# Transposed tokens made by DMA instead of TensorE, and eight score blocks moved ahead

## The chip, the core and the metric

The kernel runs on one core of one Trainium2 chip. The metric is the time of one execution on the device in microseconds (us), lower is better. A core has five engines with a queue of instructions each, which it takes in order: TensorE (PE), VectorE (DVE), ScalarE (ACT), GpSimd (POOL) and SyncE (SP, which here only issues DMAs). An instruction waits for others through semaphores, and everything behind it on its queue waits with it.

## The reference

```python
xn = layernorm(x)                                   # 2048 tokens x 512
a, b = xn @ dft_hid_re.T, xn @ dft_hid_im.T         # spectral part
y = dft_seq_re @ a - dft_seq_im @ b
q = einsum("nd,dhc->nhc", xn, w_q)                  # experts: 32 heads, two halves of 128
s1, s2 = q1 @ k1.T, q2 @ k2.T                       # 64 keys for each half
i1, i2 = the two best keys of s1 and of s2          # for each token and head
top_s, top_e = the two best of the four pairs       # index = 64 * i1 + i2, of 4096 experts
g = softmax(top_s)
act = gelu(xn . u[top_e])
out = x + y + sum over heads and experts of g * act * v[top_e]
```

All inputs and the output are f32.

## The kernel before, in words

The Python builds one straight program. The source says what is done; a scheduler of the framework puts the instructions of each engine in an order, which stays close to the source but moves small work ahead where it can run earlier. Tiles come from pools with a fixed count of buffers, and a new user of a buffer waits until the last one is done. PSUM, where matmuls write, has eight banks: four from `pa`, two from `pb`, two from `pc` (L61 to L68).

**Tokens.** The 2048 tokens lie in eight tiles of 128 partitions by 2 by 512 f32, `xp[0..7]`; `xn(g, q)` (L238) is one block of 128 tokens, and 16 blocks make four groups `g` of four. A group is two tiles, 2g and 2g+1. The same memory seen as f16 is `xt[i]` (L235): per block a high and a low part of 512 columns each, later filled with the transposed tokens. The matmuls of the experts run on two f16 parts: value times 512 (`XS`) as f16, plus what the rounding left.

**Stage 1: normalise.** `ln(g, n)` (L284) takes mean and variance of each token, works out `rstd` and `negm` (L316 to L321), and normalises the block in place on ACT or DVE. One token row of group 0 is kept aside as `x5` and normalised on POOL (L336).

**Stage 2: the spectral part along the sequence.** For each group in the order G = (1, 0, 2, 3), `fold(0, g)` (L360) adds the two tiles (L369) and folds columns (L339 to L358) into Q[0][g] (L372, L373), all on DVE with two small copies on ACT; `main(0, g)` (L394) runs eight f32 matmuls (L403) that add into the four `pa` banks. After the last group `evict(0)` copies the banks out on ACT (L455, L458). The same with differences follows: `fold(1, g)`, `main(1, g)`, `evict(1)`. `fold_row` (L375), `spread` (L385) and the end of `sides` (L438 to L441) treat the single row on POOL, with two small DMAs from POOL's queue (L389, L390); the rest of `sides` (L418) gathers two more columns on DVE.

**Stage 3: key products.** Keys and query weights don't depend on the tokens, so `m_mul` (L136) multiplies them first: for head group j, four heads, the product is `m`, 512 by 512, in four banks. `m_scale(0, ...)` (L187) takes absolute sums of the four banks, of one weight tile and of the keys on ACT (L196 to L201); `pow2` (L115) takes the maximum over all partitions on POOL (`partition_all_reduce`, L118), and DVE makes powers of two out of it (L119 to L124, L206 to L212). `m_parts` (L216) then splits `m` into two f16 parts: the high part on ACT (L219), the low part on DVE (L220), which frees the bank. The argument `at` makes `m_scale` wait for `fold(0, G[-1])`.

**Stage 4: transposes.** `xpose(i, sub)` (L469) transposes one block: four matmuls against the identity into a bank (L475), a scaled copy to f16 on ACT (L478), and the low part either as a further matmul that subtracts the rounded value inside the bank (L480, then L482 on ACT) or as one subtraction on DVE (L484). This happens between `main(1, g)` of the next groups, L549 to L561.

**Stage 5: scores and the best two.** For each of eight head groups j (`NCH`) and each of 16 blocks i, `scores(j, i)` (L773) runs 12 matmuls (L779: four columns of 128 by three products of parts) into a `pa` bank, evicts on ACT (L784), and finds the best eight values of each head with MAX8 and their indices with FIND_INDEX8 on DVE (L787, L791). What else is done between the blocks is a table: `MST0` and `MST` say behind which block each piece of `m_stage(j + 1)` (loads, key products, scale, split) goes, `sums()` (L563) stands behind block 10 of j = 0, `HID` puts the products along the hidden dimension (`y_rows`, `hid` L486) behind blocks 11 to 15 and 27 to 32, and `todo` (L799) the splits of weights (`m_prep`, L151) and the first estimates of u and v (`absmax`, `uv_scale`). During j = 1 each transposed block is also stored to DRAM (`xt_d`, L845). The weights of j are loaded by `m_load` (L131).

**Stage 6: experts.** After the eighth head group the routing is compacted by DMA transposes (L768), all 4096 experts' products with u run densely (L908), then those with v (L991), to the end. The change leaves this stage as it is.

The order of the calls around the change is L502 to L561:

```python
for n, g in enumerate(G):          # L528
    ...
    fold(0, g)
    ...
    main(0, g)
evict(0)                           # L544
m_scale(0, MS[0, "p"], FF[0, G[-1]][:, 0, 0:1])
m_parts(0, MS[0, "p"])
...
for n, g in enumerate(G):          # L549
    fold(1, g)
    ...
    main(1, g)
    if n:
        for q in range(4):
            xpose(4 * G[n - 1] + q, n < 3)
```

## Time and profile before

| what | us |
|---|---|
| median of 3 runs | 1160.65 |
| lowest and highest of them | 1159.43, 1161.57 |
| the profiled execution's own time | 1159.45 |
| span of its trace | 1157.7 |
| TensorE busy in that span | 1136.5 |
| VectorE busy | 934.5 |
| ScalarE busy | 610.6 |
| GpSimd busy | 245.0 |

The span goes from the first to the last instruction of the profiled execution; its own time is that with what lies around it. In the rows of a timeline stand the start in us, the busy time in us, the engine, the line, the operation, the tiles written and read, and how many instructions the row holds; in brackets the idle time before it and what ended that time. In a row of the DMA queues (SPq, POOLq), the three figures are the least, the median and the greatest time of an issue in ns, followed by the stretch in which they stand. In the table of stretches, each pair is the busy time of one engine and its count of instructions, in the order PE, weight loads of PE, DVE, ACT, POOL; then the granted clock of TensorE, the share of the DMA engines and GB/s.

### The profile page before, as it was taken

The page shows a single profiled execution, that of the slowest core. Times are in us where ns is not written, and L with a number is a line of the kernel's source. Part 1 is how long each engine was busy: PE and PEld are TensorE (multiplying, and loading weights), DVE is VectorE, ACT ScalarE, POOL GpSimd, SP SyncE. Part 2 cuts the span into 40 slices and gives each one's busy share as a digit, 9 for nine tenths or more (in the row PEclk, how much of TensorE's full clock was granted, in tenths as well). Part 3 has the DMA queues.
Part 4 walks back from the last instruction along what each step waited for, and adds up shares of the span by engine and source line. Part 5 has one row for each costly group of instructions (what it writes and reads, how often), then busy time and mean ns, then how long its engine had stood idle before and what let it go on. Part 6 is the DMA issues. An engine that isn't in the chain of part 4 may idle for free.

```text
span 1157.7 us, 25371 instructions
## 1 busy us (share of the span) xinstructions
PE 1136.5 (98%) x9930; PEld 724.9 (63%) x9930; DVE 934.5 (81%) x2840; ACT 610.6 (53%) x1056; POOL 245.0 (21%) x232
## 2 busy tenths in 40 slices
PE   6899999999999999999999999999999999999997
PEld 4355555445445459778478479569569559658763
DVE  7987989798898999974994895897886786788670
ACT  5575687687776635354435435535535435433440
POOL 5232464865865410000000000010010000000000
PEclk9999999999999999999999999999999999999999
DMA  9182344243241204261743743644554555451423
GB/s 364 49 294 64 124 139 169 70 164 119 83 159 52 82 11 126 87 213 37 237 157 104 229 166 107 223 159 137 186 163 169 168 174 168 155 174 56 137 75 104
DMA packets 81504, 163.64 MB, mean 141 GB/s; under 512 B 16084, under 2 KB 31323, under 8 KB 81374
## 3 DMA queue, kind: packets, MB, share of 16 engines
q1 hardware_dynamic: 81008, 161.84, 42.2%
q8 instruction: 80, 1.31, 0.5%
q14 instruction: 50, 0.41, 0.1%
q10 hardware_dynamic: 302, 0.08, 0.0%
q0 software_dynamic: 64, 0.00, 0.0%
HBM read 142.69 MB, written 17.63 MB: 138 GB/s over the span
## 4 chain that ended last, share of the span: by engine, by line
PE 93%; DVE 3%; DMA 2%; ACT 1%; issue 0%; POOL 0%; SPq 0%; ACTq 0%; POOLq 0%; DVEq 0%
PE s L779 29%; PE z L908 28%; PE v L991 27%; PE g L946 4%; PE p L403 2%; PE m L144 2%; DVE L L936 1%; PE xp L475 0%; DMA xb<-in_x_dram 0%; DMA x<-in_x_dram 0%; DMA cx<-in_wt_dram 0%; DMA fit<-v_d 0%; DVE act L962 0%; DMA y<-y_d 0%; DVE w L954 0%
## 5 line engine op out<-in xcount | busy, mean ns | idle before, releaser
L908 PE MATMUL z<-xb,u 128*128 128x256 f16 (+1 forms) x3840 | 342.9, 251 | 0.2
L991 PE MATMUL v<-v,act 128*128 128x512 f16 x1536 | 338.6, 379 | 0.0
L908 PEld LDWEIGHTS <-u 128*128 128x128 f16 x3840 | 309.8, 98 | 26.8 <-issue 0.5
L779 PE MATMUL s<-m,xq 128*128 128x512 f16 x1344 | 297.3, 379 | 0.0
L991 PEld LDWEIGHTS <-act 128*128 128x128 f16 x1536 | 147.4, 98 | 171.0
L779 PEld LDWEIGHTS <-xq 128*128 128x128 f16 x1344 | 129.6, 98 | 150.3 <-issue 0.2
L936 DVE TENSOR_TENSOR L<-io_lam,cmp 128x2048 f16<-128x2048 f16 x128 | 155.9, 1218 | 59.1 <-PE g L946 58.9
L915 ACT ACTIVATE act<-z,scl 128x256 f32<-128x256 f32 (+1 forms) x224 | 100.6, 498 | 171.5 <-PE z L908 171.4
L787 DVE MAX8 vals<-ss 128x8 f32<-128x64 f32 x1024 | 152.6, 216 | 12.6 <-ACT ss L784 12.3
L1004 POOL TENSOR_TENSOR y<-y,xr 128x512 f32<-128x512 f32 x15 | 25.2, 1679 | 611.9 <-DMA y<-y_d 455.8
L961 ACT ACTIVATE act<-w 128x1024 f16<-128x1024 f32 x52 | 69.9, 1360 | 92.8 <-DVE w L954 92.1
L791 DVE FIND_INDEX8 idx<-vals,ss 128x8 uint16<-128x256 f32 x256 | 107.2, 419 | 0.0
L954 DVE SCALAR_TENSOR_TENSOR w<-act,scl,g 128x1024 f32<-128x1024 f32 x64 | 80.9, 1274 | 29.7 <-ACT act L915 29.7
L1067 ACT ACTIVATE cx<-cx 128x896 f32<-128x896 f32 x64 | 60.5, 945 | 72.3 <-DVE cx L1047 53.7
L784 ACT ACTIVATE ss<-s,wsc 128x512 f32<-128x512 f32 x112 | 74.7, 680 | 44.3 <-PE s L779 36.6
L962 DVE TENSOR_TENSOR act<-w,act 128x1024 f16<-128x1024 f32 x64 | 84.9, 1328 | 4.2 <-ACT act L961 4.2
L1041 DVE TENSOR_TENSOR cx<-cx 128x512 f32<-128x512 f32 (+2 forms) x84 | 48.4, 610 | 28.0 <-DMA cx<-in_cb_dram 25.0
L946 PEld LDWEIGHTS <-L 128*128 128x128 f16 x2048 | 60.6, 96 | 11.2 <-DVE R L944 1.2
L946 PE MATMUL g<-R,L 128*128 128x32 f16 x2048 | 61.7, 176 | 0.2 <-DVE R L944 0.2
L944 DVE TENSOR_TENSOR R<-R,cmp 128x512 f16<-128x512 f16 x128 | 59.2, 463 | 1.5
L166 POOL TENSOR_TENSOR wq<-wq,wh 128x1024 f16<-128x1024 f32 x26 | 55.4, 2133 | 12.1 <-DVE xq L484 7.9
L941 DVE TENSOR_TENSOR R<-io_c,cmp 128x512 f16<-128x512 f16 x128 | 54.5, 426 | 0.0
(290 smaller groups left out, 1094.3 us busy)
## 6 DMA issues: line engine op xcount, KB each, us to landing
v<-v_d SPq DMA_DIRECT2D x67, 512.0 KB, 4.2
cx<-in_cb_dram SPq DMA_DIRECT2D x64, 448.0 KB, 4.7
wq<-in_wq_dram SPq DMA_DIRECT2D x32, 512.0 KB, 6.0
fit<-in_wq_dram SPq DMA_DIRECT2D x28, 512.0 KB, 5.3
...
```

The costliest lines, as they stand in the source:

```text
L779: nc.tensor.matmul(ps, xt[i][:, l, kd, :], m[:, r, kd, :], start=(n == 0), stop=(n == 3 * KD - 1))
L784: nc.scalar.activation(s.rearrange("p g e -> p (g e)"), ps, AF.Copy, scale=inv)
L787: nc.vector.max(vals[:, i, w, :, h], s[:, g, :])
L791: nc.vector.max_index(idx[:, i, w].rearrange("p k h -> p (k h)"), vals[:, i, w, 0:2].rearrange("p k h -> p (k h)"), s[:, w * HC:g + 1, :]. ...
L908: nc.tensor.matmul(ps if n == 1 else ps.rearrange("p (b n) -> p b n", b=2), ug[:, l, c % 2, kd, :], xb2[:, k0, r, kd, :] if n == 1 else xb ...
L915: nc.scalar.activation(ACT[bb][:, cg * m:cg * m + m, :], pv[:, i], AF.Gelu_apprx_tanh, scale=zsc)
L936: nc.vector.tensor_tensor(L.rearrange("p t (l two) -> p t l two", two=2), io_lam.rearrange("p (l two) -> p l two", two=2).unsqueeze(1).to_ ...
L946: nc.tensor.matmul(p[:, hf, t * NC:(t + 1) * NC], L[:, t, :], R[:, t, :], start=True, stop=True)
L954: nc.vector.scalar_tensor_tensor(w, act[:, :, ts], fw, p.rearrange("p h (n c) -> p c (h n)", c=NC), op0=ALU.mult, op1=ALU.mult)
L961: nc.scalar.activation(w16[..., 0], w, AF.Copy)
L962: nc.vector.tensor_tensor(w16[..., 1], w, w16[..., 0], op=ALU.subtract)
L991: nc.tensor.matmul(pv, w16[:, c, :, l], v_sb[g][:, r, cc, :], start=(n + cc == 0 and k == 0), stop=(n == 15 and cc == 1 and k == 2))
```

## The change

The factor 512 moves into the normalisation: `rstd` is 512 times as large, and where the spectral part leaves the banks (`turn`, `sums`, `spread`), the factor 1/512 is put into the instruction that is there anyway.

The transposes on TensorE go. `stage(i)` takes a block: ACT writes its f16 copy (with a bias of zero from `zs`, which ties it to an earlier step) into one of three staging buffers, DVE writes the difference to it, and one DMA transpose of 128 by 1024 f16, issued by SP, writes both parts to `xt[i]`. The staging buffers are `u_sb[3]` and `u_sb[4]`. The four blocks of group 1 (G[0]) are staged behind `fold(0, 0)`, those of group 0 behind `fold(1, 0)`, those of groups 2 and 3 behind `sides()`, ahead of `evict(1)`. The tokens are overwritten where the transposed tokens land, `xt[i]` in `xp[i // 2]`; for h = 2, 3 (group 1) the tokens now lie in tiles of their own.

The scale and the split of the key products (`m_scale`, `m_parts`) move from behind `evict(0)` to behind `main(0, 0)`, the second of the four sequence products. Behind them stand the first four score blocks, `early(0..3)`, in the banks of `pb` and `pc`, with an eviction on ACT into spare tiles. Four more, `early(4..7)`, stand behind `main(1, 1)`, in the same banks, without an eviction of their own. `scores(0, n)` then takes the blocks in the order TO (group 1, 0, 2, 3), and for n below 8 runs no matmuls: it evicts the bank of blocks 4 to 7 and searches the best values of all. The differences are folded in the order 0, 1, 2, 3 (GK).

Since the matmuls of the first eight blocks are gone from the list of j = 0, the other pieces move back: `MST0` puts the pieces of the key products of j = 1 behind blocks 10 to 15 (4 to 9 before), `absmax` behind 8 and 10, `uv_scale` behind 11, `m_prep` of j = 1 behind 7 to 10. The weights of j = 1 are loaded from POOL's queue, and the last two loads of difference matrices (`load(1, 2)`, `load(1, 3)`) with three small ones stand on SP behind the first four transposes.

```diff
@@ -131,7 +131,7 @@
     def m_load(j, pool, ts):
         for t in ts:
             MS[j, t] = pool(f"wq{j}_{t}")
-            nc.sync.dma_start(MS[j, t], wq[j, t // 2, t % 2])
+            (nc.gpsimd if j == 1 else nc.sync).dma_start(MS[j, t], wq[j, t // 2, t % 2])
...
@@ -238,6 +238,15 @@
     def xn(g, q):
         return xp[2 * g + q // 2][:, q % 2]
+    def s_mm(ps, m, i):
+        n = 0
+        for kd in range(KD):
+            for l, r in ((0, 0), (0, 1), (1, 0)):
+                nc.tensor.matmul(ps, xt[i][:, l, kd, :], m[:, r, kd, :], start=(n == 0),
+                                 stop=(n == 3 * KD - 1))
+                n += 1
+
+
     MP[0] = stS.enter_context(tc.tile_pool(name="mp0", bufs=1, side="left"))
...
     uf = [t.rearrange("p a b k e -> p (a b k e)").bitcast(F32) for t in u_sb]
+    EARLY = {}
+    EV = uf[7].rearrange("p (i w k h) -> p i w k h", i=NT, w=2, k=8)
+    EX = uf[4][:, 512:640].bitcast(U16).rearrange("p (i w k h) -> p i w k h", i=NT, w=2, k=2)
+    ES = uf[4][:, 640:672].rearrange("p (n c) -> p n c", n=4)
+
+    def early(n):
+
+        i = TO[n]
+        m, inv = M[0]
+        ps = (pb if n % 2 else pc)(f"s0_{i}")
+        s_mm(ps, m, i)
+        EARLY[n] = ps, None
+        if n < 4:
+            EARLY[n] = uf[5 + n // 2][:, n % 2 * 512:n % 2 * 512 + 512], ES[:, n]
+            nc.scalar.activation(EARLY[n][0], ps, AF.Copy, scale=inv)
+
     stA = ExitStack()
     da = stA.enter_context(tc.tile_pool(name="da", bufs=1, side="left"))
+    for h in (2, 3):
+        xp[h] = da.tile([P, 2, 512], F32, name=f"x{h}")
+
     def raw_tile(name):
         return da.tile([P, 2, 512], F32, tag="raw", name=name, bufs=10)
     G = (1, 0, 2, 3)
+    GK = G, (0, 1, 2, 3)
...
@@ -316,8 +347,8 @@
         nc.scalar.activation(sm[:, 0], var, AF.Sqrt, bias=eps)
         nc.vector.reciprocal(sm[:, 1], sm[:, 0])
         nc.vector.scalar_tensor_tensor(sm[:, 0], var, 1e-5, sm[:, 1], op0=ALU.add, op1=ALU.mult)
-        nc.vector.scalar_tensor_tensor(sm[:, 2], sm[:, 0], -0.5, sm[:, 1], op0=ALU.mult, op1=ALU.mult)
-        nc.vector.scalar_tensor_tensor(rstd[:, g], sm[:, 2], 1.5, sm[:, 1], op0=ALU.add, op1=ALU.mult)
+        nc.vector.scalar_tensor_tensor(sm[:, 2], sm[:, 0], -0.5 * XS, sm[:, 1], op0=ALU.mult, op1=ALU.mult)
+        nc.vector.scalar_tensor_tensor(rstd[:, g], sm[:, 2], 1.5 * XS, sm[:, 1], op0=ALU.add, op1=ALU.mult)
...
@@ -452,10 +484,10 @@
         d = turned(dst)
         v = halved(src)
         if b is None:
-            nc.scalar.activation(d, v, AF.Copy)
+            nc.scalar.activation(d, v, AF.Copy, scale=1.0 / XS)
             return
         for a in range(2):
-            nc.scalar.activation(d[..., a::2], v[..., a::2], AF.Identity, bias=b[:, a:a + 1])
+            nc.scalar.activation(d[..., a::2], v[..., a::2], AF.Identity, bias=b[:, a:a + 1], scale=1.0 / XS)
     def evict(k):
         PT[k] = [[uf[8 + 2 * k + dt][:, h * 512:(h + 1) * 512] for h in range(2)] for dt in range(2)]
...
@@ -463,25 +495,14 @@
             for h in range(2):
                 turn(PT[k][dt][h], PP[k][dt][h], s5c[:, :, dt] if h + k == 0 else None)
-    idn = cst.tile([P, P], F16, name="idn")
-    nc.gpsimd.tensor_scalar(idn, ident, -1.0 / XS, None, op0=ALU.mult)
-
-    def xpose(i, sub=False):
-
-        p = (pb if sub and i % 2 else pc)(f"xp{i}")
+    def stage(i):
+
         src = xn(i // 4, i % 4)
-        for kd in range(KD):
-            c = slice(kd * P, (kd + 1) * P)
-            nc.tensor.matmul(p[:, c], src[:, c], ident, start=kd == 0, stop=kd == KD - 1 and not sub,
-                             is_transpose=True, skip_group_check=True)
-        pv = p.rearrange("p (k n) -> p k n", k=KD)
-        nc.scalar.activation(xt[i][:, 0], pv, AF.Copy, scale=XS)
-        if sub:
-            nc.tensor.matmul(p, idn, xt[i][:, 0].rearrange("p k n -> p (k n)"), start=False, stop=True,
-                             skip_group_check=True)
-            nc.scalar.activation(xt[i][:, 1], pv, AF.Copy, scale=XS)
-            return
-        nc.vector.scalar_tensor_tensor(xt[i][:, 1], pv, XS, xt[i][:, 0], op0=ALU.mult, op1=ALU.subtract)
+        n = TO.index(i)
+        t = u_sb[3 + n % 3 // 2][:, n % 3 % 2].rearrange("p a k n -> p a (k n)")
+        nc.scalar.activation(t[:, 0], src, AF.Identity, bias=zs[:, int(n > 3):int(n > 3) + 1])
+        nc.vector.tensor_tensor(t[:, 1], src, t[:, 0], op=ALU.subtract)
+        nc.sync.dma_start_transpose(xt[i].rearrange("p a k n -> p (a k) n"), t.rearrange("p a d -> p (a d)"))
     def hid(t, n, pre, pn, pim, bank):
...
@@ -516,13 +537,9 @@
     row512(0, c5r, nc.scalar)
     nc.gpsimd.tensor_copy(c52, c5r[:, 0:2])
     nc.scalar.dma_start(c55, cb[0, 0, 0, 0:1, 8, 0:1])
-    for g in G:
+    for g in GK[1][:2]:
         load(1, g)
     wfs = uf[14][:, 0:512]
-    nc.sync.dma_start(wfs, wf)
-    nc.sync.dma_start(w2, wr[:, 0:2].to_broadcast([P, 2]))
-    row512(1, A[1, 0][0:1, 512:1024])
-
     for t in range(2):
         m_mul(0, t, (0, 1))
     for n, g in enumerate(G):
@@ -531,6 +548,15 @@
         if 0 < n < 3:
             ln(G[n + 1], n + 1)
         fold(0, g)
+        if n == 1:
+            nc.scalar.activation(zs[:, 0:1], rstd[:, g, 0:1], AF.Copy, scale=0.0)
+            for q in range(4):
+                stage(4 * G[0] + q)
+            for h in GK[1][2:]:
+                load(1, h)
+            nc.sync.dma_start(wfs, wf)
+            nc.sync.dma_start(w2, wr[:, 0:2].to_broadcast([P, 2]))
+            row512(1, A[1, 0][0:1, 512:1024])
         if n == 3:
             fold_row(0)
             spread()
@@ -541,24 +567,31 @@
                 m_mul(0, t, (2, 3))
             for t in range(2, 4):
                 m_mul(0, t, range(KD))
+        if n == 1:
+            m_scale(0, MS[0, "p"], FF[0, g][:, 0, 0:1])
+            m_parts(0, MS[0, "p"])
+            nc.scalar.activation(zs[:, 1:2], wsc[:, 0:1], AF.Copy, scale=0.0)
+            nc.scalar.activation(k16[:, 0], k_sb, AF.Copy, scale=sk)
+            nc.vector.scalar_tensor_tensor(k16[:, 1], k_sb, sk, k16[:, 0], op0=ALU.mult, op1=ALU.subtract)
+            for b in range(4):
+                early(b)
     evict(0)
-    m_scale(0, MS[0, "p"], FF[0, G[-1]][:, 0, 0:1])
-    m_parts(0, MS[0, "p"])
-    nc.scalar.activation(k16[:, 0], k_sb, AF.Copy, scale=sk)
-    nc.vector.scalar_tensor_tensor(k16[:, 1], k_sb, sk, k16[:, 0], op0=ALU.mult, op1=ALU.subtract)
-    for n, g in enumerate(G):
+    for g in GK[1]:
         fold(1, g)
         if g == 0:
             nc.vector.tensor_copy(Q[1][0][0:1, 0, 1:256], s5i[:, 1:256])
             nc.scalar.activation(xp[1][0:1], x5, AF.Copy)
+            for q in range(4):
+                stage(q)
         main(1, g)
-        if n:
-            for q in range(4):
-                xpose(4 * G[n - 1] + q, n < 3)
+        if g == 1:
+            for b in range(4, 8):
+                early(b)
     sides()
+    for g in (2, 3):
+        for q in range(4):
+            stage(4 * g + q)
     evict(1)
-    for q in range(4):
-        xpose(4 * G[-1] + q)
     def sums():
         b8 = pc("b8")
...
@@ -770,18 +803,19 @@
             nc.scalar.activation(cmp, zt.unsqueeze(3).to_broadcast([P, 3, P, 2]), AF.Copy)
             CMP[b] = cmp
-        def scores(j, i, vals, idx):
+        def scores(j, n, vals, idx):
             m, inv = M[j]
-            ps = pa(f"s{j}_{i}")
-            n = 0
-            for kd in range(KD):
-                for l, r in ((0, 0), (0, 1), (1, 0)):
-                    nc.tensor.matmul(ps, xt[i][:, l, kd, :], m[:, r, kd, :], start=(n == 0),
-                                     stop=(n == 3 * KD - 1))
-                    n += 1
-            st = sp.tile([P, 520], F32, tag="s", name=f"ss{j}_{i}", bufs=3 if safe else 4)
-            s = st[:, 0:512].rearrange("p (g e) -> p g e", g=2 * HC)
-            nc.scalar.activation(s.rearrange("p g e -> p (g e)"), ps, AF.Copy, scale=inv)
+            i = n if j or safe else TO[n]
+            ps, spare = (None, None) if j or safe else EARLY.pop(n, (None, None))
+            s = ps
+            if spare is None:
+                if ps is None:
+                    ps = pa(f"s{j}_{i}")
+                    s_mm(ps, m, i)
+                st = sp.tile([P, 520], F32, tag="s", name=f"ss{j}_{i}", bufs=3 if safe else 4)
+                s, spare = st[:, 0:512], st[:, 512:]
+                nc.scalar.activation(s, ps, AF.Copy, scale=inv)
+            s = s.rearrange("p (g e) -> p g e", g=2 * HC)
             for g in range(2 * HC):
                 w, h = divmod(g, HC)
                 nc.vector.max(vals[:, i, w, :, h], s[:, g, :])
@@ -791,10 +825,10 @@
                     nc.vector.max_index(idx[:, i, w].rearrange("p k h -> p (k h)"),
                                         vals[:, i, w, 0:2].rearrange("p k h -> p (k h)"),
                                         s[:, w * HC:g + 1, :].rearrange("p g e -> p (g e)"))
-            return st[:, 512:]
+            return spare
         MST = {1: 1, 3: 2, 5: 3, 6: 4, 8: 5, 10: 6} if safe else {3: 1, 4: 2, 5: 3, 7: 4, 8: 5, 9: 6}
-        MST0 = MST if safe else {4: 1, 5: 2, 6: 3, 7: 4, 8: 5, 9: 6}
+        MST0 = MST if safe else {10: 1, 11: 2, 12: 3, 13: 4, 14: 5, 15: 6}
         HID = {11: 8, 12: 0, 13: 1, 14: 2, 15: 3, 27: 4, 29: 5, 30: 6, 32: 7}
         todo = [[] for _ in range(NCH * NT)]
         if safe:
...
@@ -807,15 +841,15 @@
                 m_stage(0, wq_tile, t)
         else:
             am_load(0, 0)
-            for which, n in ((0, 5), (1, 9)):
+            for which, n in ((0, 8), (1, 10)):
                 todo[n].append(lambda at, w=which: absmax(w, 0, at))
-            todo[5].append(lambda at: am_load(1, 0))
-            todo[10].append(lambda at: uv_scale())
+            todo[8].append(lambda at: am_load(1, 0))
+            todo[11].append(lambda at: uv_scale())
             todo[(NCH - 1) * NT + 6].append(
                 lambda at: m_fit(NCH - 1, MP[0].tile([P, 2, KD, 512], F16, tag="m", name="mj")))
             for j in range(1, NCH):
                 for t in range(4):
-                    todo[1 + t if j == 1 else (j - 1) * NT + 2 * t - 4].append(
+                    todo[7 + t if j == 1 else (j - 1) * NT + 2 * t - 4].append(
                         lambda at, j=j, t=t: m_prep(j, t, wqp, behind(sw, at)))
         fills = [(0, g) for g in (0, 1, 2, 3, 8, 9, 10, 11, 12, 13, 14, 4, 5, 6, 7, 15)] + [(1, g) for g in range(V2)]
         slots = [29, 31, 36, 43, 45] + [16 * j + i for j in range(3, 7) for i in (4, 6, 11, 13)]
```

Left out of the diff: the factor 1/512 in `spread` and `sums`, the tile `zs`, `main` taking first and last group from GK[k], the buffers of `vals` and `idx` for j = 0, and a factor in a branch that these inputs don't take. In the changed file the lines of the parts above are: `early` L262 to L271, `turn` L487 and L490, `stage` L503 to L505, the searches L821 and L825, the store of `xt_d` L882.

22 lines of the change are left out of this document (14 added, 8 removed).

## The prediction

> **What bounds the kernel now.** The page first: shares of the engines, their busy tenths in 40 slices, and the chain that ended last.
>
> ```profile
> PE 1136.5 (98%) x9930; PEld 724.9 (63%) x9930; DVE 934.5 (81%) x2840; ACT 610.6 (53%) x1056; POOL 245.0 (21%) x232
> PE   6899999999999999999999999999999999999997
> PE 93%; DVE 3%; DMA 2%; ACT 1%; issue 0%; POOL 0%; SPq 0%; ACTq 0%; POOLq 0%; DVEq 0%
> ```
>
> TensorE (PE) is the bound: only the first two slices and the last show it less than full. So the change is worth what it takes off PE's list, less every microsecond in which it makes PE wait. The timeline of PE shows the only wait that can be filled, and the chain of waits shows what is on PE's list behind it.
>
> ```profile
> 26.51 3.70 PE L403 MATMUL p<-c,q 128*128 128x512 f32 x8 [0.45 <-DVE q L372]
> 34.37 15.90 PE L403 MATMUL p<-c,q 128*128 128x512 f32 x32 [4.16 <-DVE q L372]
> ```
>
> ```profile
> 71.11 9.50 PE s L779 x44
> ...
> 119.34 10.36 PE s L779 x48
> ```
>
> After the second sequence product PE waits 4.16 us, then runs from 34.37 to 119.34, the first score of head group 1, without a real gap: 84.97 us. That stretch is where the change acts; from 119.34 on the list is the same. So I compare one number: when does that first score of group 1 start?
>
> **What is removed.** The same chain, from 34 to 120 us (86 us), grouped by line:
>
> ```profile
> by line: PE s L779 49.3%; PE p L403 26.8%; PE xp L475 6.6%; PE m L144 3.3%; PE xp L480 2.4%; PE b L568 2.0%; PE hy L488 1.4%; ACT xq L482 1.4%; PE hy L491 1.3%; PE hy L489 1.3%; PE hy L490 1.3%; PE b L578 1.1%; ACT xq L478 0.6%; ACT xb L478
> ```
>
> The PE transposes (L475) are 6.6% and their corrections (L480) 2.4%, together 7.7 us. The ACT pieces of the same lines (some 1.7 us) are steps in which PE went on with other transposes. Between 7.7 and 9.4 us I take 9.0. Score blocks are only moved: 9.50 us for 44 matmuls is 0.216 each, 2.59 a block of 12.
>
> **What is moved: the key products now stand behind GpSimd.** In the changed program the first four score blocks stand on PE's queue between the second and third sequence products, ahead of products that do not need them. They need the scaled key products, which need the maximum over partitions on GpSimd (POOL).
>
> ```profile
> 11.09 0.24 POOL L77 IOTA iof<- 128x128 f32 x1 [10.16 <-issue]
> 17.38 4.21 POOL L336 TENSOR_SCALAR x<-x,mvs,rstd 1x512 f32<-1x512 f32 x2 [2.75 <-DVE rstd L320]
> 35.33 0.87 POOL L390 DMA_DIRECT2D s5c<-s_d  x1
> 48.29 1.15 POOL L118 PARTITION_ALL_REDUCE pw<-mx  x1 [12.09 <-ACT m L201]
> 106.50 2.86 POOL L165 TENSOR_SCALAR wq<-wq,wsc 128x1024 f32<-128x1024 f32 x1 [10.13 <-ACT wh L158]
> ```
>
> ```profile
> L77 POOLq MODIFY_POOL_CONFIG  x2: 11/11/11, 0.9 to 1.0; - x2
> ```
>
> ```profile
> L118 POOLq MODIFY_POOL_CONFIG  x4: 4/20/37, 36.5 to 81.1; - x4
> ```
>
> The maximum ran at 48.29, and the page puts its wait on ScalarE (ACT). But two things stand ahead of it on POOL, and the change moves neither: the row work of fold_row, spread and sides, unbroken from 17.38 to 36.2, and behind it a MODIFY_POOL_CONFIG at 36.5, a reload of POOL's code. What a reload costs is hidden here under 12.09 us of waiting. The one reload that stands alone is the first: issued at 1.0, next instruction at 11.09, nothing else waited for, 10.1 us. The one before L165 is bounded by 10.13. So the bounds are 0 and 10.1; I take 10.1, the only row with nothing beside it. The Trainium skill (GPSIMD Engine Reference, section Instruction dispatch) says that the first call of freshly loaded code pays some 6 us behind MODIFY_POOL_CONFIG; no row here shows 6, and with it the sum below would be 4.1 us smaller.
>
> Then the maximum runs from 46.6 to 47.75. It gains 1.7 us by the change, though its inputs are ready some 14 us sooner. From there to the first score:
>
> ```profile
> 47.77 0.29 ACT L201 ACTIVATE m<-k_sb 128x128 f16<-128x128 f32 x1
> 50.73 2.42 ACT L219 ACTIVATE m<-m,msc 128x512 f16<-128x512 f32 x4 [2.58 <-DVE wsc L209]
> ```
>
> ```profile
> 37.81 1.22 DVE L369 TENSOR_TENSOR ft<-xq,xq 128x1024 f32<-128x1024 f32 x1
> 49.47 0.17 DVE L119 TENSOR_SCALAR pw<-pw 128x3 f32<-128x3 f32 x1 [0.29 <-POOL pw L118]
> 51.45 2.72 DVE L220 SCALAR_TENSOR_TENSOR m<-m,msc,m 128x512 f16<-128x512 f32 x4
> ```
>
> L119 to L219 took 1.26 us with two 0.35 us fold steps between that no longer stand there; I take 0.75. Then one L219 (0.6), and one L220 (0.7), which the first score needs because it writes the bank that L220 empties. First score at 47.75 + 0.05 + 0.75 + 0.6 + 0.7, about 49.9. Before, PE resumed at 34.37. PE's last product now ends near 32.0 (26.51 + 3.70, plus three token subtractions of 0.6 each put ahead of it on VectorE (DVE); half of L369's 1.22). So PE stands idle some 18 us, and resumes **15.5 us later**. The 2.1 us that it lost at a granted clock below full (15.90 us for 16 products that need 0.86 each) is lost in both.
>
> What is queued behind the wait matters as much. DVE's queue has the chain L119 to L220 ahead of the folds of groups 2 and 3; before, it did those folds while it waited for the maximum. ACT has L219 ahead of the normalisation of group 3.
>
> **What is added: DMA transposes on SP.** The trace has transposes of 128x384 halves.
>
> ```profile
> L768 SPq DMA_TRANSPOSE zt<-z_d x14: 1190/1210/2287, 452.0 to 957.5; - x14
> L768 SPq DMA_TRANSPOSE zt<-z x2: 1183/1248/1312, 431.8 to 433.8; - x2
> ```
>
> ```profile
> 434.27 0.84 ACT L770 ACTIVATE cmp<-zt 128x768 f16<-128x768 f16 x1 [3.70 <-DMA zt<-z]
> ```
>
> ```profile
> 152.92 0.38 SPq L657 DMA_DIRECT2D uv<-in_ut_dram  x1
> ```
>
> A plain issue takes SP 0.38 us, a transpose of 384 columns 1.2. The new ones have 1024 columns: between 1.2 (no growth) and 3.2 (in proportion, times 8/3); a part may be fixed, so I take 3.0. The result was used at 434.27, 2.5 us after the issue began: some 1.2 behind its end, of which the data's part grows; I take 1.7. The Trainium skill (Advanced Engine Details and Errata, section X-Bar Transpose) says that transposing DMAs are as fast as plain ones; the issue rows speak against it. By that rule the queue term below would be nothing.
>
> The store of each block (L845, now L882) stands on SP behind its own transpose and waits until it has landed. A pair of blocks so takes 3.0 + 3.0 + 1.7 + 0.4, about 8 us, where PE needs 5.2. The token copies use three buffers, so ACT's copy of block n waits for the landing of block n-3, and evict(1), which frees the banks for the remaining scores, stands behind the last copy on ACT. Block 0's transpose overwrites its tokens and so waits for the fold of differences of group 0, on DVE. From L219 at 48.5: L220 2.7, two subtractions 1.2, the small steps of group 3 0.6, fold of group 2 2.3, maxima of one block 2.0, folds up to that point 4: near 62.4. SP then: three pairs to 86.4, block 10 with its store to 91.4, blocks 11 and 12 to 97.4, landed 99.1, last copy and evict: 100.2. PE's own list from 49.9 is early blocks 10.4 + 2.1 of low clock, two sum products 6.9, two difference products 6.9, four blocks 10.4, two products 6.9: 93.5. It waits **6.7 us**, split between evict(0) and evict(1), and I add **2.1** for one more restart at low clock.
>
> **DVE behind.** A block's maxima and indices cost DVE 2 us: 70.32 to 72.28.
>
> ```profile
> 70.32 0.73 DVE L787 MAX8 vals<-ss 128x8 f32<-128x64 f32 x5
> ...
> 72.28 1.27 DVE L484 SCALAR_TENSOR_TENSOR xq<-xp,xq 128x512 f16<-128x512 f32 x2
> ```
>
> ```profile
> 40.00:60.00 20.00, 19.63 (x71) 9.91 (x70) 19.47 (x54) 15.96 (x36) 1.15 (x1) 1.00 0.14 54
> 60.00:120.00 60.00, 60.00 (x400) 33.94 (x399) 48.42 (x236) 39.55 (x86) 19.96 (x9) 1.00 0.49 166
> ```
>
> In the second row DVE (third figure) is busy 48.4 of 60 us. The change saves it L484 (5.2 us, by eight of 0.65) and gives it 16 subtractions (9.6), and its 10 us or more of new waiting before 47.75 must come out of those 12 us of slack. At 100.2 it still owes some 6.5 early blocks. The key products of group 1 now occupy all four spare banks from score 10 to score 15, and sums() and the first hidden products stand behind them. They are freed by L220, behind the maxima of score 13: 100.2 + 12.5 blocks of 2 + 3.6 of other work, near 128.8. PE gets there at 100.2 + 6 scores 15.5 + key products 2.8 + score 14 2.4, that is 121. It waits **7 us** (I take a little off, since DVE does some of this while PE waits).
>
> Costed at nothing: the factor 512 in rstd and its inverse in evictions and in spread (no new instruction but a second operand); the removed idn; the two zs copies (0.2 us, ACT idle); separate tiles for group 1's tokens (their loads stay first on SP); group 1's key weights loaded by POOL behind L441: they arrive later, under DVE's delay. If that cover goes, they cost up to 2 us.
>
> **Sum.** 15.5 - 9.0 + 6.7 + 2.1 + 7.0 = +22.3 us. From 119.34 on nothing gives it back, as PE has no gaps. Against the profiled execution's own 1159.45 (span 1157.7, median of the runs 1160.65): **1181.8 us**.
>
> **Rivals.**
> - Short issue: transposes take SP 1.2 us whatever their width. Then SP keeps ahead of PE, the queue term and one restart go, and DVE, freed sooner, costs 2 to 7: 15.5 - 9.0 + 4.5, 1170. For it: one width only is in the trace. Against: 1.2 is already three times a plain issue.
> - Short reload: the reload costs half, 5 us; at the start it shared the DMA engines with loads. Everything behind it moves by 5: 1177. The rows exclude neither.
> - Faster: the reload costs next to nothing (10.1 was the start of the program). The maximum ends at 37.7, PE resumes at 39.9, 5.5 later than before, less 9.0: -3.5 us, 1156, if transposes also issue in 1.2 and DVE keeps up. It decides at a reload below 3.5 us. For it: every later reload is hidden under a wait. Against: the only free row.
> - Worse: issue in full proportion, low clock at each restart, DVE and POOL slower under shared traffic: +32, 1191.
> - The change not doing what it says: the four blocks would fill the 4.16 us. The queue order excludes it, unless the maximum is ready.
>
> **How the numbers follow.** Main case 0.45, short issue 0.16, short reload 0.18, worse 0.10, faster 0.08, no change 0.03. The range goes from 1164 (issue and reload both short: 1170 less 5, less a little) to 1192 (just above the worse case); outside lie the faster case, no change and the tails of the others, some 0.17. A measurement here can tell about 0.2% (2.3 us) from no change: faster 0.08, within 0.03, slower 0.89.
>
> **What would show it.** POOL: MODIFY_POOL_CONFIG near 36.5 and the maximum near 46.6 with its inputs long done. PE: an idle stretch of some 18 us ahead of the first early score. SP: transposes of about 3 us, pairs some 8 us apart. ACT: stage copies waiting for DMA, evict(1) near 100. First score of group 1 near 142. Wrong, if the maximum comes before 40, or PE's idle time behind 50 us is small.

## The result, and the profile after

| | before | changed |
|---|---|---|
| median of 4 runs, us | 1161.11 | 1170.41 |
| lowest and highest | 1159.43, 1161.80 | 1169.94, 1171.74 |
| span of the profiled execution, us | 1157.7 | 1168.8 |

The ratio is 1.0084, 95% interval 1.0067 to 1.0102: slower by 9.3 us, where 21.2 had been forecast (1181.8 against the median before that was known then, 1160.65). Direction and range held; the size was more than twice too large. First the page of the changed kernel: shares of the engines, PE's busy tenths and granted clock in 40 slices, and the chain that ended last.

```profile
PE 1133.7 (97%) x9858; PEld 720.1 (62%) x9858; DVE 934.9 (80%) x2848; ACT 607.4 (52%) x1050; POOL 247.8 (21%) x235
PE   5598999999999999999999999999999999999997
PEclk9798899999999999999999999999999999999999
PE 75%; DVE 15%; POOL 4%; issue 2%; DMA 2%; ACT 1%; POOLq 0%; SPq 0%; DVEq 0%; ACTq 0%
```

The first five slices (29 us each) hold it all: apart from the last slice, as before, busy tenths and clock fall below 9 only there. Of the chain, 93% was PE before; now it is 75%, with VectorE and GpSimd on it. The timeline of PE in that stretch (in brackets the idle time and what ended it):

```profile
28.05 5.09 PE L435 MATMUL p<-c,q 128*128 128x512 f32 x8 [2.55 <-DVE q L403]
44.90 12.02 PE L245 MATMUL s<-m,xq 128*128 128x512 f16 x48 [11.75 <-DVE m L220]
...
66.86 4.56 PE L435 MATMUL p<-c,q 128*128 128x512 f32 x10 [0.50 <-DVE fo L382]
...
96.81 0.22 PE L144 MATMUL m<-sums,wh 128*128 128x64 f16 x2 [0.40 <-issue]
100.20 0.23 PE L144 MATMUL m<-sums,wq 128*128 128x64 f16 x1 [3.17 <-POOL wq L166]
...
116.44 1.95 PE L601 MATMUL b<-w,u 128*128 128x2 f32 x16 [0.39 <-DVE m L220]
...
129.97 5.34 PE L245 MATMUL s<-m,xb 128*128 128x512 f16 x24
```

PE resumes at 44.90 instead of 34.37, 10.5 us later. The first score of group 1 (129.97; in the chain 130.14 against 119.34) comes 10.8 us later. From there on the two run alike, to spans 11.1 us apart. Between, the table of stretches (the first pair is PE, the third figure from the end the granted clock):

```profile
44.00:48.00 4.00, 3.10 (x8) 1.13 (x8) 3.88 (x10) 3.77 (x11) 0.00 (x0) 0.50 0.67 146
48.00:96.00 48.00, 47.50 (x173) 21.07 (x171) 46.94 (x165) 21.68 (x37) 9.48 (x6) 1.00 0.74 194
96.00:100.00 4.00, 0.63 (x4) 0.13 (x2) 2.75 (x18) 4.00 (x7) 1.98 (x1) 0.90 1.03 412
100.00:106.00 6.00, 5.80 (x33) 2.81 (x34) 5.45 (x27) 3.61 (x8) 2.26 (x2) 0.50 0.95 359
119.00:127.00 8.00, 8.00 (x40) 6.01 (x39) 3.66 (x19) 2.93 (x16) 7.72 (x3) 0.57 0.00 1
```

From 48 to 96 us PE is busy 47.50 of 48 us: nothing of what had been forecast for that stretch is there. Three losses stand in its place behind 96: a wait of 3.6 us (0.40 and 3.17), 5.80 us of work at a granted clock of 0.50 (2.9 lost), and 8.00 us at 0.57 (3.4 lost) behind a wait of only 0.39.

### The profile page after: what moved, and what is told of

Its sections match the earlier page's. It is cut to its first block, busy times and chain, and to the rows that moved or that the text cites. A ratio compares the mean times of both kernels' runs of the same rounds, so it can differ in the third digit from the quotient of the medians.

```text
span 1168.8 us, 25265 instructions
## 1 busy us (share of the span) xinstructions
PE 1133.7 (97%) x9858; PEld 720.1 (62%) x9858; DVE 934.9 (80%) x2848; ACT 607.4 (52%) x1050; POOL 247.8 (21%) x235
## 4 chain that ended last, share of the span: by engine, by line
PE 75%; DVE 15%; POOL 4%; issue 2%; DMA 2%; ACT 1%; POOLq 0%; SPq 0%; DVEq 0%; ACTq 0%
PE v L1028 27%; PE z L945 26%; PE s L245 15%; PE g L983 4%; DVE vals L821 4%; DVE idx L825 3%; PE m L144 1%; PE p L435 1%; POOL wq L165 1%; DVE L L973 1%; POOL wq L166 1%; DVE z L763 1%; DVE act L999 1%; DMA wq<-in_wq_dram 1%; DVE ft L400 1%
## 5 line engine op out<-in xcount | busy, mean ns | idle before, releaser
L245 PE MATMUL s<-m,xq 128*128 128x512 f16 x1344 | 301.7, 383 | 11.8 <-DVE m L220 11.8
L821 DVE MAX8 vals<-ss 128x8 f32<-128x64 f32 x896 | 133.5, 217 | 5.0 <-ACT ss L817 4.7
L998 ACT ACTIVATE act<-w 128x1024 f16<-128x1024 f32 x52 | 69.9, 1361 | 96.5 <-DVE w L991 95.9
L825 DVE FIND_INDEX8 idx<-vals,ss 128x8 uint16<-128x256 f32 x224 | 93.9, 419 | 0.0
```

The lines of the kernel that those rows point to most:

```text
L245: nc.tensor.matmul(ps, xt[i][:, l, kd, :], m[:, r, kd, :], start=(n == 0), stop=(n == 3 * KD - 1))
L821: nc.vector.max(vals[:, i, w, :, h], s[:, g, :])
L825: nc.vector.max_index(idx[:, i, w].rearrange("p k h -> p (k h)"), vals[:, i, w, 0:2].rearrange("p k h -> p (k h)"), s[:, w * HC:g + 1, :]. ...
L998: nc.scalar.activation(w16[..., 0], w, AF.Copy)
```

## The experiments

Two theories. **A**: what costs is the place of the early scores, behind the maximum on GpSimd. **L**: what costs behind 96 us is the key weights of group 1, late because their load waits for the memory that the last sequence product reads, and the banks that they then hold. The rival of both is **B**: VectorE stood idle for 10.5 us (31.9 to 42.5) and its lag comes up wherever the slack is least. Each run stands beside runs of the kernel before on the same chip. The chips differ from round to round (the kernel before has medians from 1161.14 to 1162.50 us there), so runs of different rounds are compared by their ratios.

| run | median us | ratio to before | 95% |
|---|---|---|---|
| e1 maximum first | 1166.14 | 1.0044 | 1.0027 to 1.0061 |
| e2 scale and early scores late | 1166.80 | 1.0041 | 1.0027 to 1.0056 |
| e3 early scores 4 to 7 last | 1174.91 | 1.0118 | 1.0101 to 1.0135 |
| e4 key products one later | 1166.60 | 1.0049 | 1.0033 to 1.0066 |
| e5 sums and hidden first | 1175.90 | 1.0123 | 1.0106 to 1.0140 |
| e6 e1, bias later | 1168.09 | 1.0053 | 1.0035 to 1.0070 |
| e7 e5 and e6 | 1171.41 | 1.0083 | 1.0066 to 1.0100 |
| e8 DMA transposes alone | 1169.15 | 1.0058 | 1.0037 to 1.0078 |
| e9 e5, group 2 later | 1167.93 | 1.0058 | 1.0039 to 1.0076 |
| e10 e7, group 2 later | 1164.35 | 1.0026 | 1.0016 to 1.0037 |
| e11 transposes halved | 1180.37 | 1.0161 | 1.0141 to 1.0181 |
| e12 e1, e5, group 2 later | 1166.85 | 1.0045 | 1.0029 to 1.0061 |
| e13 e10, weights by GpSimd | 1164.80 | 1.0023 | 1.0011 to 1.0034 |
| e14 e9, weights by GpSimd | 1170.46 | 1.0062 | 1.0044 to 1.0080 |
| e15 e13, routing off GpSimd | 1162.52 | 1.0007 | 0.9998 to 1.0015 |
| e16 e14, routing off GpSimd | 1167.47 | 1.0050 | 1.0036 to 1.0064 |
| e17 e15, group 2 one later | 1160.53 | 0.9985 | 0.9974 to 0.9996 |

**e1, the maximum first.** A copied cell ties the row work to the maximum:

```diff
+        if not k:
+            nc.gpsimd.tensor_copy(r[:, 0, 0:1], PW[0])      # PW[0]: a cell of the maximum
         nc.gpsimd.tensor_tensor(r[:, 0, 0:512], x5[:, 0], x5[:, 1], op=ALU.subtract if k else ALU.add)
```

> The changed kernel with one copy on GpSimd that ties the row work to the maximum, so that the maximum over partitions stands ahead of the row work (only its two normalisations stay ahead of it). Theory A (the maximum waits on GpSimd for row work and reload, and PE waits for the maximum): the reload now falls into idle time, the maximum runs near 33.8 us instead of 42.1, the first early score starts near 36.5 instead of 44.9, and the time falls by about 8 us, to 1162. Rival B (VectorE is what is late behind the maximum, so an earlier maximum only moves the wait to the next fold): the first score starts earlier all the same, but PE then waits at the third sequence product, and the time falls by 4 us at most, to 1166.

4.3 us faster than the changed kernel, half of what A promised, and the 1166 that B gave. Its PE timeline, then GpSimd's:

```profile
34.44 12.21 PE L247 MATMUL s<-m,xq 128*128 128x512 f16 x48 [3.55 <-DVE m L222]
58.58 9.25 PE L439 MATMUL p<-c,q 128*128 128x512 f32 x16 [4.67 <-ACT u L494]
```

```profile
31.63 0.40 POOL L118 PARTITION_ALL_REDUCE pw<-mx  x1 [10.33 <-ACT m L202]
39.88 1.27 POOL L413 TENSOR_TENSOR r<-x 1x512 f32<-1x512 f32 x1 [7.20 <-issue]
```

The first early score stands at 34.44, 10.5 us earlier, as at PE's old resumption: that the maximum's place delays PE is shown. But the row work now ends late, the eviction of the first banks needs it, and PE waits 4.67 us there: for ScalarE behind GpSimd, not for VectorE's fold as B had it. GpSimd's second row shows a reload again: done with the maximum and its copy at 32.7, it needs 7.20 us until its next addition starts.

**e2, scale and early scores late.** The second block under `if n == 1:` (scale, split, first four early scores) under `if n == 3:`.

> The changed kernel with the whole block of scale, split and first four early scores moved back behind the fourth sequence product; DMA transposes, early scores 4 to 7 and all else as changed. Theory A (the early place behind GpSimd cost 10.5 us at PE's resumption): PE resumes near 34.4 us at the third sequence product, and the time falls by 8 to 10 us, to 1161. Rival C (the DMA transposes, the staging and the late weights are the cost): the time stays within 3 us of the changed kernel, above 1167.

3.6 us faster, not 8 to 10. PE's timeline:

```profile
35.82 3.70 PE L435 MATMUL p<-c,q 128*128 128x512 f32 x8 [2.42 <-DVE q L403]
41.69 3.70 PE L435 MATMUL p<-c,q 128*128 128x512 f32 x8 [2.17 <-DVE q L403]
47.53 6.23 PE L435 MATMUL p<-c,q 128*128 128x512 f32 x10 [2.14 <-ACT u L490]
```

PE resumes at 35.82 and then waits for VectorE's fold or ScalarE's eviction in front of each sequence product, and later still 3.17 us for the weights of group 1 and 1.85 ahead of the sums. Both theories get a part: the place costs, and so does what follows it.

**e3, early scores 4 to 7 behind the last sequence product; e4, the key products of group 1 one block later** (`MST0` from {10: 1, ...} to {11: 1, 12: 2, 13: 3, 14: 4, 15: 5 and 6}).

> The changed kernel with early scores 4 to 7 behind the last sequence product instead of behind the second of the differences, so that the last sequence product, whose matrices the key weights of group 1 overwrite in memory, ends some 10 us sooner. Theory L (these weights arrive late because their load waits for that product): the load is issued near 84 us instead of 89.3 (then GpSimd's queue is the limit), PE's wait of 3.2 us ahead of the key products of group 1 and the 3 us at low clock behind it go, and the time falls by 5 to 6 us, to 1165. Rival D (VectorE's backlog decides when the key products of group 1 can be used, the late weights are covered by it): the wait goes but comes back ahead of the sums, 1169 to 1171.

> The changed kernel with the key products of group 1 one score block later each (behind blocks 11 to 14, scale and split both behind 15). Theory L (late weights): PE has 2.6 us more work ahead of them, its wait falls from 3.2 us to under 1, the low clock behind it may go or stay; the time falls by 2.5 to 5.5 us, to 1165 to 1168. Rival D (VectorE's backlog): the split is later too, the banks come free later, the wait ahead of the sums grows from 0.4 to 3 us and takes the gain back: 1169 to 1172.

e3 was 4.5 us slower, against both. Its last sequence product ended at 77.8 us, and the load still came at 87.87: GpSimd was free at 83.8, and the load then followed the last staging copy on ScalarE (86.54 to 87.26), which reads the zero column `zs` in the same freed memory. So two uses of that memory end within 2 us, and L's detail (the product alone) is wrong. What PE lost more is mainly the wait ahead of the sums, 4.50 us for L220 in place of 0.39: rival D of that expectation. That the load waited for the zero column was not tried by itself. e4 was 3.8 us faster: no wait for the weights, clock 1.00 throughout from 96 to 127, but waits of 1.53 and 2.27 us where the hidden products and the key products now share banks.

**e5, sums and hidden products first; e9, the same with the weight copies of group 2 later.**

```diff
-        HID = {11: 8, 12: 0, 13: 1, 14: 2, 15: 3, 27: 4, 29: 5, 30: 6, 32: 7}
+        HID = {8: 8, 9: 0, 10: 1, 25: 2, 26: 3, 27: 4, 29: 5, 30: 6, 32: 7}
-                if j == 0 and i == 10 and not safe:
+                if j == 0 and i == 7 and not safe:          # sums()
...
-                    todo[7 + t if j == 1 else (j - 1) * NT + 2 * t - 4].append(
+                    todo[7 + t if j == 1 else NT + t if j == 2 else (j - 1) * NT + 2 * t - 4].append(   # e9
```

> The changed kernel with the sums (behind block 10) moved to the end of the search of block 7, and the first hidden products behind blocks 8, 9 and 10 (25, 26 for two of them) instead of 11 to 15: PE then has them ahead of the key products of group 1, not behind their banks. Theory L (the late weights, and the banks that the key products hold until VectorE splits them, cost two waits and two stretches at half clock, together 10 us): the wait of 3.6 us ahead of the key products and that of 0.4 ahead of the sums go, with the half clock from 100 to 106 and from 119 to 126.5; the time falls by 6 to 9 us, to 1163. Rival S (the half clock belongs to the sums themselves, whose matmuls are tiny, wherever they stand): only the first wait and its stretch go, 3 to 5 us, 1166.

> The kernel of e5 with the f16 copies of the weights of group 2 behind blocks 0 to 3 of group 1 instead of behind 12 and 14 of group 0 and 0 and 2 of group 1, so that on ScalarE they stand behind the split of the key products of group 1. In e5 PE had no wait and no half clock from 48 to 119 us, and then waited 10.7 us for that split, which stood behind a copy that waited for its weights. Theory L (late weights and held banks cost the changed kernel some 10 us): the wait of 10.7 goes, the first score of group 1 starts near 119 to 121 and the time is 1160 to 1163. Rival M (the late weights of group 2 stop PE wherever their copy stands): the wait comes back as a full set of score banks in group 1, 1168 or more.

e5 was 5.5 us slower; PE had no wait of note from 48 to 119 us, then:

```profile
130.09 0.58 PE L245 MATMUL s<-m,xb 128*128 128x512 f16 x1 [10.74 <-ACT m L219]
```

The split (L219) stood on ScalarE behind the copy of group 2's first weights, which waited 16.74 us for their load. e9 took the copies out of the way: first score of group 1 at 118.66 instead of 129.97, of which 1.8 us are two hidden products moved behind it; clock 1.00 from 80 to 120. The 9.5 us that are left are close to the 10.3 that L's waits and low clock had cost, so L names the place. Rival S is not settled. The sums and hidden products stand in the same order in both runs, without a wait ahead of them, but in e5 the granted clock was 0.65 from 92.5 to 96.5 us, in e9 1.00. The same hidden product, first in e5, then in e9:

```profile
94.90 0.63 PE L510 MATMUL hy<-u,u 128*1 128x128 f32 x2
```

```profile
94.45 0.38 PE L510 MATMUL hy<-u,u 128*1 128x128 f32 x2
```

So e5 did have a stretch at low clock behind the sums, against what the expectation of e9 says of it. And the time of e9 was only 2.5 us below the changed kernel (ratios 1.0058 and 1.0084):

```profile
133.99 0.20 PE L144 MATMUL m<-sums,wq 128*128 128x64 f16 x1 [3.65 <-POOL wq L166]
```

```profile
108.51 6.24 SPq L635 DMA_DIRECT2D y_d<-u  x1
114.85 5.26 SPq L634 DMA_DIRECT2D y_d<-u  x1
120.27 1.85 SPq L134 DMA_DIRECT2D wq<-in_wq_dram  x4
```

The weights of group 2 stand on SP behind stores whose issues took 6.24 and 5.26 us. Rival M of that expectation: the wait comes back one group later.

**e6, e1 with the row's part added after the eviction; e7, e6 and e5 together; e10, e7 with e9's shift; e12, e10 without the later bias.**

```diff
-                turn(PT[k][dt][h], PP[k][dt][h], s5c[:, :, dt] if h + k == 0 else None)
+                turn(PT[k][dt][h], PP[k][dt][h])
+    def bias():                                             # called ahead of sides()
+        for dt in range(2):
+            d = turned(PT[0][dt][0])
+            for a in range(2):
+                nc.scalar.activation(d[..., a::2], d[..., a::2], AF.Identity, bias=s5c[:, a:a + 1, dt])
```

> The kernel of e1 (maximum ahead of the row work) with the row's contribution added to the evicted tiles afterwards on ScalarE, so that the eviction of the first four banks no longer waits for the row work. In e1 PE waited 4.67 us for that eviction at 58.58 us. Theory A (the maximum's place costs 10.5 us of which e1 gave back 4.67 and a restart at half clock): the wait goes, the time falls by 4 to 6 us below e1, to 1161. Rival B (VectorE's folds are as late as the eviction): less than 2 us below e1, 1165.

> e6 and the sums and hidden products first, together. If the two causes (maximum behind the row work; late weights with held banks) are separate and add up: 4 for e1, 4 to 6 for the bias, 6 to 9 for the order, 1151 to 1156, faster than the kernel before by 0.5% or more. If VectorE, busy over 90% up to 80 us, bounds both: 1160.

> The kernel of e7 (maximum first, bias later, sums and hidden products first) with the same shift of group 2's weights. If the two causes add up: the first score of group 1 starts near 115 us (125.5 less the wait of 11.0 that e7 had there), 4 to 5 us ahead of the kernel before, and the time is 1154 to 1158. If VectorE bounds it: no better than e9, 1160 to 1163.

> e10 without the later bias: the first four banks are evicted only when the row work is through, as in e1 (a wait of 4.7 us at 58.6 us, in place of three of 1.6 to 2.1 in e6). e1 was 2 us faster than e6. If that holds here: 1153 to 1157, 1 to 2 us below e10. If the bias later pays once the other waits are gone: 1 to 3 us above e10.

e6 was no faster than e1. PE's timeline shows the 4.67 us in pieces elsewhere:

```profile
50.40 3.70 PE L439 MATMUL p<-c,q 128*128 128x512 f32 x8 [1.81 <-DVE q L405]
55.72 1.10 PE L439 MATMUL p<-c,q 128*128 128x512 f32 x2 [1.62 <-ACT u L491]
58.88 8.02 PE L439 MATMUL p<-c,q 128*128 128x512 f32 x14 [2.07 <-ACT u L491]
95.04 0.23 PE L145 MATMUL m<-sums,wq 128*128 128x64 f16 x1 [3.09 <-POOL wq L167]
112.35 3.57 PE L612 MATMUL b<-w,u 128*128 128x2 f32 x16 [2.92 <-DVE m L222]
```

That is rival B. e7 had e5's stall (10.96 us for the split), so its time says nothing on whether the parts add up; e10 is that test: first score of group 1 at 111.68 us, 18.3 before the changed kernel's (1.8 of it again the two hidden products), but 6.1 us gained in time, not 12 to 16: behind it PE waits 0.90 us for the split and 3.53 for the weights of group 2, and the clock is 0.83 from 120 to 140. e12 was 2.5 us above e10 on the same chip: with the other waits gone, the later bias pays, where e1 and e6 (ratios 1.0044 and 1.0053) can't be told apart.

**e8, the DMA transposes alone:** no early scores, tables and queue of the weights as before.

> The changed kernel without early score blocks: scale and split behind the fourth sequence product, all 16 blocks scored behind the last eviction, key products, sums and estimates behind the blocks where the kernel before has them, weights of group 1 loaded by SP. What is left of the change is the factor 512, the staging and the DMA transposes. Theory A' (the transposes by DMA pay, the early blocks behind GpSimd are what costs): PE loses 9 us of work and waits less than 5 us more for folds, 1156 or less. Rival C (the PE transposes filled time in which PE waits for VectorE's folds anyway): PE's waits between the products are 2 us or more each, as in e2, and the time is 1160 to 1166.

1169.15, against both expectations, 7 us above the kernel before. PE waits ahead of the products as in e2 (2.31, 2.43, 2.18, 2.14), and then:

```profile
80.84 7.67 PE L245 MATMUL s<-m,xb 128*128 128x512 f16 x24 [6.20 <-DMA xt_d<-xq]
```

The row names a store, but ScalarE's rows at that place show what PE waited for:

```profile
79.30 0.72 ACT L503 ACTIVATE u<-xq,zs 128x512 f16<-128x512 f32 x1 [0.61 <-DMA xq<-u]
80.10 1.26 ACT L813 ACTIVATE ss<-s,msc 128x512 f32<-128x512 f32 x2
```

Four score blocks had filled the four banks, and the first bank's eviction (begun at 80.10, PE goes on at 80.84) stood behind the last staging copy, which waited until a transpose gave its buffer back. With no other work for PE, this chain of copies and transposes on three buffers costs 6.20 us. The early scores are what hides it in the changed kernel, so they are not a cost alone. That TensorE's own transposes had filled time in which PE would else wait for folds is not shown: all four waits lie ahead of 47.4 us, and in the kernel before, which waits 0.45 and 4.16 us in that part, the transposes begin only at 52.27.

**e11, each transpose in two halves.**

```diff
-        nc.sync.dma_start_transpose(xt[i].rearrange("p a k n -> p (a k) n"), t.rearrange("p a d -> p (a d)"))
+        for a in range(2):
+            nc.sync.dma_start_transpose(xt[i][:, a], t[:, a])
```

> The changed kernel with each DMA transpose of 1024 columns as two of 512. Issue theory F (an issue costs SP 1.2 to 1.33 us whatever its width): each block now takes 2.5 us, a pair with its stores over 7 us, and SP is where the prediction had put it with 3.0 us each: then the queue step of the prediction can be seen at work, PE waits 4 to 7 us ahead of the last evictions, 1175 to 1178. Issue theory P (in proportion, above a small fixed part): two halves cost as much as a whole, time unchanged within 2 us.

10 us slower. The DMA issues of the line, first in the changed kernel, then in e11 (least, median, greatest ns):

```profile
L505 SPq DMA_TRANSPOSE xq<-u x14: 1245/1301/3894, 22.5 to 87.8; - x14
```

```profile
L506 SPq DMA_TRANSPOSE xq<-u x28: 1190/1264/2912, 20.9 to 97.8; - x28
```

1.30 us for 1024 columns, 1.26 for 512, 1.2 for the 384 of the last stage: the price is per issue. With two issues a block SP takes 2.5 us, near the 3.0 that the prediction had given it, and the time rises by 10 us where the queue step had 8.8. But PE pays elsewhere: 0.91 us in front of a sequence product, then 2.66, 4.05 and 1.03 us at the key products of group 1, whose load went out at 90.77, behind the last sequence product (done at 90.08).

**e13 and e14, group 2's weights on GpSimd's queue** (`nc.gpsimd if j in (1, 2)`) in e10 and e9; **e15 and e16**, group 0's first routing operations on VectorE and four blocks later in those two; **e17**, e15 with group 2's key products one block later, hidden products 2 to 6 behind blocks 27 to 31 and each store of hidden rows one block sooner.

> The kernel of e10 with the weights of group 2 loaded by GpSimd's queue instead of SP's, where they stood behind stores of the hidden rows whose issues took up to 6.2 and 5.3 us each. e10 had its first score of group 1 at 114.9 us, 4.4 us ahead of the kernel before (119.34), and then a wait of 3.5 us for these weights and a stretch at half clock. Theory L (the two causes, and then this third late load, are all that stands against the change): wait and half clock go, the kernel ends 3 to 6 us earlier than e10, 1158 to 1161, equal to the kernel before or up to 0.3% faster. Rival B (VectorE's backlog from the first 80 us is what surfaces in one wait after the other): a wait of 2 us or more appears elsewhere between 115 and 160 us, and the time stays at 1162 to 1165.

> The kernel of e9 with the same change of queue for the weights of group 2: only the order behind 88 us is changed against the changed kernel, the maximum stays behind the row work. e9 had the first score of group 1 at 120.2 us, 9.8 us ahead of the changed kernel, and lost 4.5 us of waits and a stretch at half clock to these weights. Theory L: the time falls to 1161 to 1163, 8 to 9 us below the changed kernel, with no change to the part ahead of 88 us. Rival B: a new wait of 2 us or more in its place, 1165 to 1168.

> The kernel of e13 with the six routing operations of group 0 that stood on GpSimd ahead of the weights of group 2 moved to VectorE, and the routing four blocks later. In e13 GpSimd held these weights, landed by 117 us, behind the first routing operation, which waited until 122.66 for VectorE's last searches of group 0; PE then waited 4.16 and 1.53 us. Theory B2 (VectorE's lag reaches PE through GpSimd's queue, here and nowhere else): both waits go and the half clock with them, 1157 to 1160 where e13 had 1164.8. Rival B (VectorE's lag finds the next place: the split of group 2, the banks of the scores): a wait of 2 us or more elsewhere before 200 us, 1163 or more.

> The kernel of e14 with the same move of the routing. VectorE lags more here, since it still waited for the maximum to 42.5 us. Theory B2: the waits of 3.48 and 1.09 us go, 1162 to 1165 where e14 had 1170.5. Rival B: 1168 or more, with a wait elsewhere.

> The kernel of e15 with the key products of group 2 one score block later (behind blocks 4 to 8 of group 1 instead of 3 to 7, scale and split behind 9 and 10), and the hidden products 2 to 6 behind 27 to 31. In e15 the last waits behind 60 us were 2.80 and 0.32 us for the weights of group 2, with a stretch at a granted clock of 0.91 over 120 to 140 us. Theory B2 (late weights at this one place): PE has 2.6 us more work ahead, waits and low clock go, the time falls by 3 to 5 us to 1158 to 1160, 0.1 to 0.3% below the kernel before. Rival B (VectorE's lag): a wait elsewhere, 1162 or more.

e13 and e14 gained nothing: their ratios, 1.0023 and 1.0062, are those of e10 and e9 (1.0026 and 1.0058) within the intervals. GpSimd in e13:

```profile
108.91 2.34 POOL L135 DMA_DIRECT2D wq<-in_wq_dram  x4
122.66 0.31 POOL L761 TENSOR_TENSOR c<-u 128x64 f32<-128x64 f32 x1 [11.40 <-DVE idx L836]
122.97 2.85 POOL L166 TENSOR_SCALAR wq<-wq,wsc 128x1024 f32<-128x1024 f32 x1
```

The weights were issued at 108.91, and stood ready behind a routing operation that waited for VectorE's last search of group 0: VectorE's lag, by way of another queue. e15 and e16 moved that operation and landed between their two expectations, with ratios lower by 0.16% and 0.12%; for e16 that is within the intervals. The waits of 4.16 and 1.53 us for these weights shrank to 2.80 and 0.32 in e15; in e16 one of 3.46 us stayed. e17 gained more (ratio 0.9985 after 1.0007) and is 0.15% faster than the kernel before, with the interval just clear of no change. The longest of what it still waits for behind 34 us:

```profile
34.72 10.52 PE L247 MATMUL s<-m,xq 128*128 128x512 f16 x48 [3.40 <-DVE m L222]
50.49 3.70 PE L439 MATMUL p<-c,q 128*128 128x512 f32 x8 [1.82 <-DVE q L405]
58.94 8.02 PE L439 MATMUL p<-c,q 128*128 128x512 f32 x14 [2.14 <-ACT u L491]
116.58 3.18 PE L247 MATMUL s<-m,xb 128*128 128x512 f16 x14 [0.84 <-DVE m L222]
133.43 0.20 PE L145 MATMUL m<-sums,wq 128*128 128x64 f16 x1 [2.00 <-POOL wq L167]
```

In its first 60 us PE is busy 40.67 us against 45.64 before. There half of the saved transposes goes, into waits for the split, folds and evictions that have become late. VectorE is busy 50.19 of those 60 us, against 51.44 before: it is not busier there, but its folds come later. It is not settled whether a further version could win them, since none tried relieves VectorE itself.

## Why the prediction was wrong, step by step

| step | forecast us | measured us |
|---|---|---|
| PE resumes later | +15.5 | +10.5 |
| transposes removed | -9.0 | -10.1 (what is left) |
| queue of transposes on SP, with a restart at low clock | +8.8 | +0.5 (the only wait there, put down to a fold on VectorE) |
| low clock at PE's resumption | 0 | -0.4 |
| VectorE behind, banks held | +7.0 | +3.8 (0.39 wait, 3.4 at low clock behind it) |
| key weights of group 1 | 0, "up to 2" | +6.5 (3.6 wait, 2.9 at low clock) |
| sum to the first score of group 1 | +22.3 | +10.8 |

Waits are rows of PE's timeline; the low clock is busy time times what is missing of the clock. The -0.4: the 48 early score matmuls took 12.02 us where 48 take 10.36 at full clock, 1.7 lost against 2.1 before. The removed work is the remainder and takes in the errors of the other rows.

Three terms failed, then: the reload at 10.1 us (it took 5.96), the queue of transposes at 8.8 (0.5), and the key weights at nothing (6.5). Two were too large and one too small, so that the time lies in the range, and at the 1170 of the rival "Short issue", is partly luck: that rival kept the long reload, and with issue and reload both short the prediction had 1165. By the sign that the prediction had named itself, PE's idle time behind 50 us, it was wrong too: 4.5 us of waits up to the first score of group 1, where it had 13.7.

- **What bounds, and where to look: right.** Only the stretch up to the first score of group 1 changed.
- **"I take 10.1, the only row with nothing beside it": the mis-sized term.** GpSimd in the changed kernel:

```profile
34.93 0.87 POOL L422 DMA_DIRECT2D s5c<-s_d  x1
42.09 0.40 POOL L118 PARTITION_ALL_REDUCE pw<-mx  x1 [6.28 <-issue]
```

  and its chain of waits at that place:

```profile
36.13 5.96 issue
```

  The maximum's inputs were complete at 33.9 us and it waited, as forecast, for row work and reload, but the reload took 5.96 us. So the 10.1 us at the start of the program are no measure of a later reload; what else they hold is not shown. Row work ending 0.4 earlier, 0.40 us instead of 1.15 for the reduction and 2.41 instead of 2.15 to the first score make up 44.90. "Short reload" was the right rival here. The Trainium skill (GPSIMD Engine Reference, section Instruction dispatch) has some 6 us for the first call of freshly loaded code; this row agrees, and the sum by it would have been 1177.7.
- **"a part may be fixed, so I take 3.0": wrong.** Nearly all of it is fixed: 1.30 us for 1024 columns, 1.26 for half of them (e11). Three pairs of SP's transposes in the changed kernel, with the stores of each pair between them left out:

```profile
57.17 2.66 SPq L505 DMA_TRANSPOSE xb<-u  x2
62.18 2.67 SPq L505 DMA_TRANSPOSE xq<-u  x2
67.11 2.67 SPq L505 DMA_TRANSPOSE xq<-u  x2
```

  A pair every 5.0 us, not 8; PE needs 5.2. So the 8.8 did not come. (The step had an error of its own as well: from L219 at 48.5 its terms add up to 61.3, not to "near 62.4".) The Trainium skill (Advanced Engine Details and Errata, section X-Bar Transpose) would have put this term at nothing, and that is what it was here, although an issue costs 1.30 us against 0.36 for the plain store behind it (L882, median). The rival "Short issue" named this. The chain of copies and transposes is real all the same: e8 shows it uncovered (6.20 us), and e11, with 2.5 us of issue a block, costs 10 us, though mostly by way of the weights.
- **"VectorE behind ... 7 us": place right, size wrong.** PE does wait for L220 ahead of the sums, 0.39 us. The forecast counted VectorE's lag from the last eviction at 100.2; the last staging copy ended at 86.7 and that eviction, right behind the last product, at 89.3, so VectorE had more room. The low clock behind that short wait was not in the forecast, and its cause is open: e5 had one at the sums without any wait, e4 and e9 had none.
- **"Costed at nothing: ... group 1's key weights": wrong, the largest miss on the other side.** The cover was gone and the price was 6.5 us, not 2. I had placed the loads behind L441 on GpSimd and had not asked which memory they land in:

```profile
83.48 0.72 POOL L473 TENSOR_TENSOR u<-u,r 1x257 f32<-1x257 f32 x1
89.34 2.33 POOL L134 DMA_DIRECT2D wq<-in_wq_dram  x4 [5.15 <-ACT u L487]
```

  GpSimd was ready at 84.2 and the load went out at 89.34, behind the last sequence product (81.61 to 88.64) whose memory it takes over. The row puts the wait on the eviction of that product; but in e1, e2, e4, e10 and e11 too the load stands 0.69 to 0.70 us behind the end of the product, and in e11 ahead of the end of the last eviction (91.04). Only three score blocks stand between that product and the first key product. e4 puts one more between them, and the wait and the low clock behind it are gone. In the kernel before the same load went out on SP 14.7 us ahead of the first key product (80.45):

```profile
65.76 1.76 SPq L134 DMA_DIRECT2D wq<-in_wq_dram  x4
```

- **What is late next:** each cause that was taken away alone gave back about half of the 9.3 us at most (e1 4.3, e2 3.6, e4 3.8), because VectorE's folds, ScalarE's evictions, the weights of group 1, then those of group 2 were next. This is rival B as far as e6, e10 and e13 show it. Only with all of them together was the kernel before reached (e15, ratio 1.0007) and passed by 0.15% (e17).
